# Moving two scatters of token numbers behind an early gather in a fused attention, SwiGLU and top-1 mixture-of-experts kernel

## The chip, the cores and the metric

The kernel runs on one core of a Trainium2 chip. The metric is device time in microseconds (us); lower is better. Before the change three runs took 1044.61, 1042.28 and 1041.61 us, so the median is 1042.28 us.

## The reference

Three layers follow one another: causal attention with a cumulative decay (4 batches, 8 heads, 576 positions, 64 per head), a SwiGLU layer on 2304 tokens of width 512 with 1536 inner columns, and a mixture of 8 experts in which each token goes to one expert. What matters here is the third:

```python
def _moe2_ref(x, w_gate, w1, w2):
    logits = x @ w_gate
    expert_idx = np.argmax(logits, axis=1)
    ...
    gate_w = probs[np.arange(N), expert_idx]
    for e in range(E):
        mask = expert_idx == e
        ...
        xe = x[mask]
        h = np.maximum(xe @ w1[e], 0.0)
        ye = h @ w2[e]
        out[mask] = gate_w[mask, None] * ye
```

## The kernel before

Phase 1 computes attention and, in between, the SwiGLU layer in nine groups of 256 tokens (`NG` = 9, group numbers 0 to 8). A group has six units. A unit `u` is `unit_g` (24 matmuls into `g`), `unit_v` (24 matmuls into `v`), and, one unit later, `unit_o` (12 matmuls into `yp`). Between them ScalarE makes `t` (L514) and `hi` (L530), VectorE makes `t` (L517, L524), and GpSimd makes `lo` (L531), which the last matmuls of `unit_o` read.

When a group is complete, `fin0` copies `yp` to `ys` and writes it to the DRAM table `y_d` (L562), `fin1` turns it, and `fin2` finds each token's expert and its rank there. `fin2` adds the token's number to a table `ixf` of 320 places per expert (three tiles of 128, 128 and 64 places). Tokens beyond 320 go to an overflow list `id_d` in DRAM: `fin2` computes places `pos` (L726) and token numbers `tid` (L728), and `put_ids` (L736) stores them with two indirect DMAs from GpSimd (L738), one for each half of the group. Places beyond the table's end are dropped by the bounds check. `pos` and `tid` are tiles of the pool `rt`, which has one buffer for each name, so the next group's `tid` has to wait until the scatters have read the last one's.

After `fin2` of group 7 (`NG - 2`), expert 0's first tile of 128 tokens is known. `early_tile` (L966) converts its 128 token numbers to `ix0` (L969) and gathers their rows from `y_d` into `xg` with an indirect DMA from GpSimd (L1051). Two units later, in the midst of the last unit's `v` matmuls, TensorE transposes those rows into `px` (L1062), and the last group's `fin1` and `fin2` are filled with expert 0's matmuls on that tile (`filler`, L990).

Phase 2 then runs the experts one by one: gathers of the token rows (L1051), first matmul (L1177), second (L1220), scatter to the output (L983). Weights come in pieces of 512 KB through four buffers `wr` (load L939 on the queue of SP, split on ScalarE L948 and VectorE L949 into a high and a low part).

The order of instructions on each engine is set by the framework's scheduler from the order of the code and a time model. `tc.keep_in_program_order` and `tc.issue_after` bind an instruction to its place, or to a place behind another instruction. GpSimd, like each engine, works through its own list in order: an instruction that waits holds all behind it. The second scatter of a pair waits until the first has landed, because both write `id_d`.

For the last group (8) the scatters are put off: `pos` and `tid` are copied to tiles of the pool `x0` (L731, L732) and stored in phase 2 (L1337).

Of the kernel before, what the change touches and what calls it, by code (L numbers as in the profile page):

```python
# [11 lines left out]
I32 = mybir.dt.int32  # L12
# [3 lines left out]
ALU = mybir.AluOpType  # L16
# [11 lines left out]
def kernel(  # L28
# [25 lines left out]
    NG = NT // G  # L54
# [4 lines left out]
    NSLOT = NE * OVS  # L59
    MAXOV = (NT - CAP + 127) // 128  # L60

    vec, act, pe, sp, gp = nc.vector, nc.scalar, nc.tensor, nc.sync, nc.gpsimd
# [417 lines left out]
    last = {}  # L480
# [135 lines left out]
    def fin2(g):  # L616
        yt, lg = ytp.pop(g)
        ps = ps_s.tile([128, 512], F32, tag="s", name="ps")
        for kk in range(KD):
            pe.matmul(  # L620
                out=ps[32 * kk:32 * kk + 32, 0:G], lhsT=rg[:, kk, :], rhs=yt[:, :, kk, :], start=True, stop=True,
# [6 lines left out]
        for i in range(2):  # L628
            pe.matmul(
                out=ps[:, NE * i:NE * i + NE], lhsT=lgp[:, 128 * i:128 * i + 128], rhs=sel, start=True, stop=True,  # L630
                skip_group_check=True,
            )
        rt = M["rt"]
# [7 lines left out]
        for i in range(2):  # L641
            vec.scalar_tensor_tensor(
                out=oh0[:, i, :], in0=lgv[:, i, :], scalar=mx[:, i, :], in1=desc, op0=ALU.is_ge, op1=ALU.mult
# [5 lines left out]
        for c0, m, i, first, last_ in (  # L649
# [4 lines left out]
                out=rk[:, c0:c0 + NE], lhsT=m, rhs=oh[:, i, :], start=first, stop=last_, skip_group_check=True  # L654
# [3 lines left out]
        for i in range(2):  # L658
            vec.tensor_tensor_reduce(
                out=junk[:, i, :], in0=cnt, in1=oh[:, i, :], scale=1.0, scalar=0.0, op0=ALU.mult, op1=ALU.add,  # L660
# [4 lines left out]
        for i in range(2):  # L665
            vec.tensor_tensor_reduce(
                out=junk[:, i, :], in0=rk[:, NE * i:NE * i + NE], in1=oh[:, i, :], scale=1.0, scalar=cs[:, i, :],
# [13 lines left out]
            out=eq, in0=slotc.rearrange("p (o s) -> p o s", o=1).to_broadcast([128, 2, NT3]),  # L681
# [4 lines left out]
            out=ra, in0=iota.rearrange("p (o t) -> p o t", o=1).to_broadcast([128, 2, 128]),  # L686
# [35 lines left out]
        )  # L722
        vec.tensor_tensor(out=pb_, in0=pb_, in1=rank, op=ALU.add)
        vec.tensor_tensor(out=pb_, in0=pb_, in1=ov_, op=ALU.mult)
        pos = rt.tile([128, 2, 1], I32, tag="pos", name="pos")
        vec.tensor_single_scalar(out=pos, in_=pb_, scalar=float(NSLOT), op=ALU.add)  # L726
        tid = rt.tile([128, 2], I32, tag="tid", name="tid")
        vec.tensor_single_scalar(out=tid, in_=tokm[:, 2 * g:2 * g + 2], scalar=float(NT), op=ALU.add)  # L728
        if g == NG - 1:
            EP["ids"] = [EP["x0"].tile([128, 2], I32, name=x) for x in ("pos8", "tid8")]  # L730
            vec.tensor_copy(out=EP["ids"][0], in_=pos.rearrange("p i o -> p (i o)"))  # L731
            vec.tensor_copy(out=EP["ids"][1], in_=tid)  # L732
        else:
            put_ids(pos.rearrange("p i o -> p (i o)"), tid)

    def put_ids(pos, tid):  # L736
        for i in range(2):
            gp.indirect_dma_start(  # L738
                out=id_d[:, :], out_offset=bass.IndirectOffsetOnAxis(ap=pos[:, i:i + 1].bitcast(U32), axis=0),
                in_=tid[:, i:i + 1], in_offset=None, bounds_check=NSLOT - 1, oob_is_err=False,  # L740
            )
# [331 lines left out]
    def unit(u, between=None):  # L1073
        if u < NU:
            t = unit_g(u)
            if between:
                between()
            unit_v(u, t)
        if u > 0:
            if u - 1 < NJ:  # L1080
                upto(markw[u - 1])
            unit_o(u - 1)
            g1, j1 = divmod(u - 1, NJ)
            if g1 == NG - 1 and j1 < len(EP["w2"]):
                EP["w2"][j1]()
                if j1 == len(EP["w2"]) - 1:
                    EP["w1"] = [go() for go in load_w(1, 1, w1[1])]
            if j1 == NJ - 1:
                if g1 == 0:
                    sg.close()  # L1090
                    M.update(routing_pools())
                fin0(g1)
                if g1 == NG - 1:
                    fill.append(filler())
                late.extend([(u + 1, fin1, g1), (u + 2, fin2, g1)])
        for x in list(late):
            if x[0] <= u or u == NU:
                x[1](x[2])
                late.remove(x)
                if x[1] == fin2 and x[2] == NG - 2:  # L1100
                    early_tile()
                    late.append((u + 2, lambda xs: transp(xts[0], 0, xs, lambda _: ps_x.tile(
                        [128, 512], F32, tag="x", name="px"
                    )), EP["xs"]))
# [212 lines left out]
    for s in range(NE + 1):  # L1317
        nxt = s + 1 if s < NE else None
        if s == 2:
            table()  # L1320
            reg["e"] = nc.values_load(
                tabi[0:1, 0, 0:1], engines=[mybir.EngineType.SP], min_val=0, max_val=NE - 1
            )
            reg["r"] = nc.values_load(
                tabi[0:1, 1, 0:1], engines=[mybir.EngineType.SP], min_val=0, max_val=NSLOT - 128
            )
            sp.dma_start(out=ixo, in_=id_d[bass.ds(reg["r"], 128), :])
            gp.indirect_dma_start(
                out=gwo, out_offset=None, in_=g_d[:, :],
                in_offset=bass.IndirectOffsetOnAxis(ap=ixo.bitcast(U32), axis=0),  # L1330
            )
        if nxt is not None:
            xgs[nxt] = fetch_x(nxt)
        if s == 1:
            pos_l = ix_p.tile([128, 2], I32, name="pos_l")
            tc.keep_in_program_order(vec.tensor_copy(out=pos_l, in_=EP["ids"][0]))
            put_ids(pos_l, EP["ids"][1])  # L1337
        live = [go() for go in weights(nxt, 1)] if nxt is not None and s else []
        if s < NE:
            h = ht_p.tile([128, KF2, 2 * CAP], F32R, tag="h", name="h")  # L1340
            for fk in range(KF2):
                mm1(fk, wt[s, 1], xts[s % 2], bank, h, 0 if s else 128)
                if fk >= 4 and live:
                    live.pop(0)()
        for f_ in live:
            f_()
        live = [go() for go in weights(nxt, 2)] if nxt is not None else []
        if nxt is not None:
            if nxt == 1:
                transp(xts[1], 0, xgs[1], bank)  # L1350
            else:
                turn(xts[nxt % 2], xgs[nxt])
        if nxt == NE:
            h_ov = [
                x.rearrange("p k c -> p (k c)")[:, 0:1024].rearrange("p (k c) -> p k c", k=KF2) for x in xts[s % 2]
            ]
            hs = hs_p.tile([128, KD, CAP], F32, tag="hs", name="hs").rearrange("p k c -> p (k c)")[:, 0:1024]
            mm1s(wt[NE, 1], xts[NE % 2], bank, hs, *h_ov)
        todo = [(t, n, idx) for t, (_, n, idx) in enumerate(xgs[s]) if s or t]
        for t, n, idx in todo:  # L1360
            mm2(t, n, idx, gate(s, t), wt[s, 2], *((h, h[:, :, LO:]) if s < NE else h_ov), bank, o_p)
            if live:
                live.pop(0)()
        for f_ in live:
            f_()
# [4 lines left out]
    with tc.tile_pool(name="lw", bufs=1) as lw, tc.tile_pool(name="lr", bufs=3) as lr, tc.tile_pool(  # L1370
        name="lx", bufs=1
# [67 lines left out]
```

## Time and profile before

| | us |
|---|---|
| median of three runs | 1042.28 |
| the profiled execution, its time | 1036.55 |
| its span from the first to the last instruction | 1034.8 |
| TensorE busy in it | 885.4 (86%) |
| GpSimd busy in it | 397.6 (38%) |
| last units of phase 1, routing and early tile | 726 to 777 |

Times in the rows are microseconds from the span's start. A row of a timeline has the start, the length, the engine, the line and the operation, and in brackets the idle time of its engine just before it with what ended it. PE is TensorE, PEld its weight load, DVE VectorE, ACT ScalarE, POOL GpSimd, SP the engine whose queue issues plain DMAs. An indirect DMA's row on POOL is the time in which GpSimd writes it out; its data land later. Ends of matmuls are modelled, so neighbouring rows overlap a little.

### The profile page before, as it was taken

What the parts mean: (1) busy time and instruction counts of PE and PEld (TensorE: products, weight loads), DVE (VectorE), ACT (ScalarE), POOL (GpSimd) and SP (SyncE); (2) the same over time, 40 slices, a digit from 0 to 9 for tenths busy, and PEclk for the clock granted to TensorE, in tenths of its full rate; (3) what the DMA queues carried; (4) which work ended last, traced back from release to release, by engine and by line L of the source; (5) the groups of instructions that cost most, each with busy time, mean ns of one, the idle gap of its engine ahead of it and who ended that gap; (6) DMA issues with size and microseconds to landing.
All of it is one profiled execution on the core that took longest, in us unless ns stands there. A gap on an engine that the chain in (4) does not pass through costs nothing.

```text
span 1034.8 us, 19815 instructions
## 1 busy us (share of the span) xinstructions
PE 885.4 (86%) x7003; PEld 738.0 (71%) x7029; DVE 632.2 (61%) x1829; ACT 558.0 (54%) x1208; POOL 397.6 (38%) x473
## 2 busy tenths in 40 slices
PE   1545557989889988899899999999789899999995
PEld 0333436867667776788688878888668799899894
DVE  6999879497577575567765443234326787656440
ACT  5987988476576565556554231213225455555441
POOL 1567767364255234344444222222225643111101
PEclk9995557999999998999999999999898899999998
DMA  8897997258776768566754440203329987754430
GB/s 241 201 225 209 227 193 167 85 131 156 139 154 142 168 113 161 115 110 150 105 109 108 113 123 2 41 2 83 51 35 219 273 239 214 207 170 152 149 104 33
DMA packets 314409, 145.30 MB, mean 140 GB/s; under 512 B 279649, under 2 KB 292065, under 8 KB 314308
## 3 DMA queue, kind: packets, MB, share of 16 engines
q1 hardware_dynamic: 310016, 133.63, 55.7%
q0 software_dynamic: 4096, 10.24, 3.9%
q8 instruction: 56, 0.92, 0.4%
q14 instruction: 45, 0.37, 0.2%
q10 hardware_dynamic: 196, 0.14, 0.1%
HBM read 81.62 MB, written 10.31 MB: 89 GB/s over the span
## 4 chain that ended last, share of the span: by engine, by line
PE 42%; DMA 7%; issue 6%; ACT 3%; DVE 2%; POOL 2%; SPq 1%; POOLq 0%; DVEq 0%; ACTq 0%
PE bank L1220 9%; PE bank L1177 8%; PE yp L544 8%; PE v L491 7%; PE g L491 6%; DMA pair<-yt 1%; DMA out_dram<-o,ix 1%; POOL xg L1051 1%; PE px L381 1%; DMA qkt<-qks 1%; DMA pt<-p 1%; DMA pair<-words 1%; ACT st L321 1%; DMA wr<-in_moe_w_dram 1%; DVE st L311 1%
## 5 line engine op out<-in xcount | busy, mean ns | idle before, releaser
L491 PE MATMUL v<-xr,wv 128*128 128x256 f16 x1296 | 162.4, 281 | 0.0
L491 PE MATMUL g<-xr,wg 128*128 128x256 f16 x1296 | 161.4, 278 | 0.5 <-DMA xr<-xs 0.5
L491 PEld LDWEIGHTS <-wg 128*128 128x128 f16 x1296 | 123.6, 100 | 26.8 <-issue 9.2
L491 PEld LDWEIGHTS <-wv 128*128 128x128 f16 x1296 | 128.9, 101 | 18.9 <-issue 1.0
L346 POOL TENSOR_TENSOR p<-st,p 128x128 f16<-128x128 f32 (+3 forms) x128 | 108.7, 854 | 79.1 <-issue 52.4
L531 POOL TENSOR_TENSOR lo<-t,hi 128x512 fp32r<-128x512 f32 x54 | 71.5, 1324 | 148.6 <-ACT hi L530 123.4
L321 ACT ACTIVATE st<-st,nb,c 128x64 f32<-128x64 f32 (+4 forms) x160 | 102.6, 643 | 1.2
L381 PE MATMUL px<-vs,pt 128*128 128x64 f16 x1280 | 58.7, 203 | 41.0 <-DMA pt<-p 30.0
L343 DVE CAST p<-st 128x64 f16<-128x64 f32 (+4 forms) x160 | 71.8, 464 | 30.7 <-ACT st L321 21.9
L381 PEld LDWEIGHTS <-pt 128*128 128x128 f16 x1280 | 52.4, 106 | 52.4 <-DMA pt<-p 35.1
L514 ACT ACTIVATE t<-g,gscale 128x512 f32<-128x512 f32 (+3 forms) x72 | 39.3, 571 | 75.5 <-PE g L491 75.5
L256 PE MATMUL ps<-qkt 128*128 128x64 f16 (+2 forms) x192 | 56.7, 311 | 25.9 <-DMA qkt<-qks 11.3
L357 POOL TENSOR_TENSOR p<-st,p 128x64 f16<-128x64 f32 (+1 forms) x128 | 54.2, 425 | 61.5 <-DVE p L343 30.6
L1220 PE MATMUL bank<-whi,h 128*128 128x512 f32 x200 | 66.9, 400 | 4.8 <-ACT h L1182 4.8
L983 POOL DMA_INDIRECT out_dram<-o,ix x24 | 26.6, 1110 | 113.8 <-ACT o L1222 71.2
L311 DVE CUSTOM_DVE_ANT_0 st<-ps,zero 128x64 f32<-128x64 f32 (+3 forms) x160 | 55.6, 376 | 24.2 <-PE ps L264 21.0
L517 DVE SCALAR_TENSOR_TENSOR t<-t,g 128x512 f32<-128x512 f32 x54 | 36.9, 684 | 54.3 <-ACT t L514 54.2
L530 ACT ACTIVATE hi<-t 128x512 fp32r<-128x512 f32 x54 | 33.8, 625 | 60.8 <-DVE t L524 60.8
L949 DVE TENSOR_TENSOR wlo<-wr,whi 128x1024 fp32r<-128x1024 f32 x48 | 57.7, 1245 | 14.1 <-ACT whi L948 12.3
L257 PE MATMUL ps<-qkt 128*128 128x64 f16 (+2 forms) x192 | 59.9, 315 | 0.0
L544 PE MATMUL yp<-wohi,hi 128*128 128x512 f32 x144 | 59.7, 414 | 0.0
L1177 PE MATMUL bank<-xh,whi 128*128 128x320 f32 (+1 forms) x192 | 58.9, 309 | 0.5 <-ACT xh L93 0.5
(300 smaller groups left out, 2274.2 us busy)
## 6 DMA issues: line engine op xcount, KB each, us to landing
wr<-in_moe_w_dram SPq DMA_DIRECT2D x72, 512.0 KB
vr<-in_v_dram SPq DMA_DIRECT2D x16, 288.0 KB
qk_in<-in_q_dram SPq DMA_DIRECT2D x32, 128.0 KB
qk_in<-in_k_dram SPq DMA_DIRECT2D x32, 128.0 KB
v_in<-in_v_dram SPq DMA_DIRECT2D x32, 128.0 KB
y_d<-ys SPq DMA_DIRECT2D x6, 512.0 KB
wg<-in_moe_w_gate_dram SPq DMA_DIRECT2D x5, 512.0 KB
raw<-in_moe_w_val_dram SPq DMA_DIRECT2D x5, 512.0 KB
```

What stands on the lines that cost most here:

```text
L257: pe.matmul(out=ps[:, o:o + n], lhsT=lq, rhs=qkt[:, 2, k0:k1], start=False, stop=False, skip_group_check=True)
L311: vec.tensor_tensor_reduce(out=sts[m][:, k0 - 64:k1 - 64], in0=ps[:, o:o + n], in1=zero.to_broadcast([128, n]), scale=1.0, scalar=init, op ...
L321: act.activation(out=sts[m], in_=sts[m], func=ACTF.Exp, scale=c[:, 0:1], bias=nb[:, m:m + 1], accum_out=sm[:, m, hh:hh + 1],)
L343: vec.tensor_copy(out=flat[:, o + 64:o + 64 + n], in_=src)
L346: gp.tensor_tensor(out=flat[:, o1:o1 + n - 64], in0=src[:, 64:n], in1=flat[:, o + 128:o + 64 + n], op=ALU.subtract)
L381: pe.matmul(out=px[:, 128 * m + 64 * hh:128 * m + 64 * hh + 64], lhsT=pm[:, o + ph * last + c, :], rhs=vs[:, hh, c, vh, :], start=(c == 0 ...
L491: pe.matmul(out=ps[:, fi, :], lhsT=w16[:, j, kk, wi, 128 * fi:128 * fi + 128], rhs=xr[:, kk, x0:x0 + 2, xi, :], start=(n_ == 0), stop=(n_ ...
L531: last["lo"] = gp.tensor_tensor(out=lo, in0=t, in1=hi.bitcast(F32), op=ALU.subtract)
L544: pe.matmul(out=yps[g][i], lhsT=hx[:, fi, 128 * i:128 * i + 128], rhs=wo[fk][wx], start=(j == 0 and n_ == 0), stop=(j == KF // 2 - 1 and n ...
L949: (eng or vec).tensor_tensor(out=l_, in0=t, in1=h_.bitcast(F32), op=ALU.subtract)
L1177: pe.matmul(out=p, lhsT=w[wi][:, kk, 128 * fk:128 * fk + 128], rhs=x[xi][:, kk, c0:CAP], start=(n_ == 0), stop=(n_ == 3 * KD - 1),)
L1220: pe.matmul(out=p[0:m, :], lhsT=hx, rhs=wx, start=(n_ == 0), stop=(n_ == len(prods) - 1))
```

## The change

For groups 7 and 8, `pos` and `tid` get tiles of their own in the pool `x0` and are no longer copied. Group 7's `put_ids` is no longer called in `fin2`, but after `fin0` of group 8, and bound behind the last `lo` of phase 1.

```diff
-        pos = rt.tile([128, 2, 1], I32, tag="pos", name="pos")
-        vec.tensor_single_scalar(out=pos, in_=pb_, scalar=float(NSLOT), op=ALU.add)
-        tid = rt.tile([128, 2], I32, tag="tid", name="tid")
+        held = g >= NG - 2
+        pos, tid = [
+            EP["x0"].tile([128, 2], I32, name=f"{x}{g}") if held else rt.tile([128, 2], I32, tag=x, name=x)
+            for x in ("pos", "tid")
+        ]
+        vec.tensor_single_scalar(
+            out=pos.rearrange("p (i o) -> p i o", o=1), in_=pb_, scalar=float(NSLOT), op=ALU.add
+        )
         vec.tensor_single_scalar(out=tid, in_=tokm[:, 2 * g:2 * g + 2], scalar=float(NT), op=ALU.add)
-        if g == NG - 1:
-            EP["ids"] = [EP["x0"].tile([128, 2], I32, name=x) for x in ("pos8", "tid8")]
-            vec.tensor_copy(out=EP["ids"][0], in_=pos.rearrange("p i o -> p (i o)"))
-            vec.tensor_copy(out=EP["ids"][1], in_=tid)
+        if held:
+            EP["ids", g] = (pos, tid)
         else:
-            put_ids(pos.rearrange("p i o -> p (i o)"), tid)
+            put_ids(pos, tid)
...
                 fin0(g1)
                 if g1 == NG - 1:
+                    with tc.issue_after(last["lo"].ins):
+                        put_ids(*EP["ids", NG - 2])
                     fill.append(filler())
...
-            tc.keep_in_program_order(vec.tensor_copy(out=pos_l, in_=EP["ids"][0]))
-            put_ids(pos_l, EP["ids"][1])
+            tc.keep_in_program_order(vec.tensor_copy(out=pos_l, in_=EP["ids", NG - 1][0]))
+            put_ids(pos_l, EP["ids", NG - 1][1])
```

On GpSimd, from the last copies of group 7 to the gathers of phase 2 (`lo` is a unit's low part, `id_d` a scatter of token numbers, the first `xg` the early tile's gather, the later ones those of phase 2), the list before reads:

```order
L531 TENSOR_TENSOR lo<-t,hi 128x512 x3
L738 DMA id_d<-tid,pos 16384x1 x2
L531 TENSOR_TENSOR lo<-t,hi 128x512
L1051 DMA xg<-y_d,ix_9793 128x512
L1237 IOTA thr 1x128
L1242 IOTA ii 1x128
L531 TENSOR_TENSOR lo<-t,hi 128x512
L1051 DMA xg<-y_d,ix 128x512
L1051 DMA xg<-y_d,ix 64x512
```

The same stretch of GpSimd's list with the change (three to five lines further down in the file):

```order
L531 TENSOR_TENSOR lo<-t,hi 128x512 x4
L1054 DMA xg<-y_d,ix_9787 128x512
L1242 IOTA thr 1x128
L1247 IOTA ii 1x128
L531 TENSOR_TENSOR lo<-t,hi 128x512
L741 DMA id_d<-tid_9783,pos_9782 16384x1 x2
L1054 DMA xg<-y_d,ix 128x512
L1054 DMA xg<-y_d,ix 64x512
```

The two scatters have left the place in front of the fourth `lo` and the early gather, and stand behind the fifth `lo`, in front of the first gather of phase 2.

On VectorE, around the conversion of the early tile's token numbers (`ix`) at the end of group 7's `fin2`, the list before reads:

```order
L717 TENSOR_TENSOR ixf<-ixf,rk 128x48
L969 CAST ix_9793<-ixf 128x1
L972 COPY gw_9796<-ixf 128x1
L728 TENSOR_SCALAR tid<-tokm 128x2
L732 COPY tid_10218<-tid 128x2
L949 TENSOR_TENSOR wolo<-wr,wohi 128x1024
L517 SCALAR_TENSOR_TENSOR t<-t,g 128x512
```

The same place of VectorE's list with the change:

```order
L717 TENSOR_TENSOR ixf<-ixf,rk 128x48
L972 CAST ix_9787<-ixf 128x1
L975 COPY gw_9790<-ixf 128x1
L952 TENSOR_TENSOR wolo<-wr,wohi 128x1024
L517 SCALAR_TENSOR_TENSOR t<-t,g 128x512
```

The last group's `tid` and its copy are gone from here; both held `tid` now stand some 170 instructions earlier on VectorE, around the `memset` of `xg` (L1049 before), and the copy of `pos` (L731) is gone too. The lists of TensorE, ScalarE and SP hold the same instructions in the same order.

## Rows read from the trace of the kernel before

**Rows 1.** Page, part 1: busy time, share of the span and instructions of each engine.
```profile
PE 885.4 (86%) x7003; PEld 738.0 (71%) x7029; DVE 632.2 (61%) x1829; ACT 558.0 (54%) x1208; POOL 397.6 (38%) x473
```

**Rows 2.** Waits of TensorE, 726 to 780: us in total, times, longest us.
```profile
PE px L1062 <- DMA xg<-y_d,ix: 6.7, 1, 6.7
PE bank L1062 <- DMA xg<-y_d,ix: 4.1, 1, 4.1
```

**Rows 3.** Timeline of TensorE, last unit's `v` and the early transposes.
```profile
738.50 2.02 PE L491 MATMUL v<-xr,wv 128*128 128x256 f16 x17
747.21 1.12 PE L1062 MATMUL px<-ident,xg 128*128 128x128 f32 x4 [6.70 <-DMA xg<-y_d,ix]
```

**Rows 4.** Timeline of GpSimd, 726 to 770.
```profile
730.71 1.05 POOL L738 DMA_INDIRECT id_d<-tid,pos  x1 [3.16 <-DVE eq L680]
739.94 0.97 POOL L738 DMA_INDIRECT id_d<-tid,pos  x1 [8.18 <-DMA id_d<-tid,pos]
740.93 1.28 POOL L531 TENSOR_TENSOR lo<-t,hi 128x512 fp32r<-128x512 f32 x1
742.37 1.06 POOL L1051 DMA_INDIRECT xg<-y_d,ix  x1 [0.16 <-issue]
...
751.42 1.27 POOL L531 TENSOR_TENSOR lo<-t,hi 128x512 fp32r<-128x512 f32 x1 [0.98 <-ACT hi L530]
769.18 0.98 POOL L1051 DMA_INDIRECT xg<-y_d,ix  x1 [16.49 <-DVE cnt L706]
```

**Rows 5.** The chain that ended last, in order of time: start, us, what.
```profile
713.01 2.62 PE v L491 x24
715.63 2.76 PE yp L544 x12
...
742.37 4.79 DMA xg<-y_d,ix
...
747.21 1.12 PE px L1062 x4
748.33 1.49 PE v L491 x7
749.82 7.10 PE yp L544 x24
...
757.70 2.83 DMA y_d<-ys
```

**Rows 6.** Timeline of VectorE, 734 to 750.
```profile
734.62 0.15 DVE L969 CAST ix<-ixf 128x1 int32<-128x1 f32 x1
...
744.03 0.17 DVE L728 TENSOR_SCALAR tid<-tokm 128x2 int32<-128x2 f32 x1 [9.20 <-DMA id_d<-tid,pos]
...
744.31 1.22 DVE L949 TENSOR_TENSOR wolo<-wr,wohi 128x1024 fp32r<-128x1024 f32 x1
745.45 0.68 DVE L517 SCALAR_TENSOR_TENSOR t<-t,g 128x512 f32<-128x512 f32 x1
749.00 0.69 DVE L93 TENSOR_TENSOR xl<-px,xh 128x512 fp32r<-128x512 f32 x1 [2.87 <-ACT xh L93]
```

**Rows 7.** Timeline of ScalarE, 733 to 740.
```profile
733.63 0.63 ACT L530 ACTIVATE hi<-t 128x512 fp32r<-128x512 f32 x1 [2.66 <-DVE t L524]
736.06 1.06 ACT L948 ACTIVATE wohi<-wr 128x1024 fp32r<-128x1024 f32 x1 [1.81 <-PE yp L544]
```

**Rows 8.** Stretches: length, busy us of each engine, PEclk (granted clock), DMA share, GB/s.
```profile
716.00:720.00 4.00, 4.00 (x30) 2.77 (x29) 2.23 (x4) 1.86 (x3) 1.27 (x1) 1.00 0.45 131
...
730.00:739.00 9.00, 9.00 (x71) 7.70 (x70) 2.88 (x14) 2.61 (x4) 1.05 (x1) 1.00 0.57 58
...
747.21:752.95 5.74, 5.74 (x19) 4.63 (x20) 1.44 (x2) 1.23 (x2) 1.80 (x3) 0.50 0.22 78
772.73:776.92 4.19, 0.07 (x1) 0.03 (x1) 0.18 (x1) 0.44 (x1) 3.06 (x4) 1.00 0.58 128
776.92:783.80 6.88, 6.40 (x31) 5.89 (x31) 4.88 (x6) 5.55 (x8) 4.37 (x4) 0.51 0.83 244
```

## The prediction

> **What bounds the kernel now.** I read the page first: TensorE is busy for 885.4 us, 86% of the span [rows 1], so time can be won only where it stands still or runs slowly. The list of TensorE's waits between 726 and 780 then shows two holes, 6.7 us before the early tile's transposes and 4.1 us before those of phase 2, both ended by a gather's landing [rows 2]. The change touches the first. TensorE's timeline places it: 17 of the 24 `v` matmuls of the last unit end at 738.50 + 2.02 = 740.52, and the transposes that stand next in its list start at 747.21 [rows 3].
>
> Why the gather is late stands in GpSimd's timeline [rows 4]. The first scatter is written out at 730.71 to 731.76; the second waits 8.18 us for its landing and is written at 739.94 to 740.91; the `lo` behind it runs from 740.93, and the gather follows at 742.37. The chain of waits takes the same way: gather 4.79 us from issue to landing, transposes, `v`, 24 `yp`, `ys`, and the write of `y_d` [rows 5]. The gather's own input was ready long before: `ix` was converted at 734.62 to 734.77 [rows 6]. So the scatters, which nobody needs soon, hold up a gather on which TensorE stands.
>
> The hole has a second price. The granted clock was 0.50, the level of 1.2 GHz, through the 5.74 us after it [rows 8]. The chain shows this in durations: 24 `yp` took 7.10 us there, where 12 took 2.76 at full clock, and 7 `v` took 1.49 where 24 took 2.62 [rows 5].
>
> **The change part by part.** *Scatters out of the gather's way.* GpSimd's list now has `lo`, `lo`, gather. The `lo` in front of the gather needs `hi`, which ScalarE ends at 733.63 + 0.63 = 734.26 [rows 7]. With 0.1 us to pass on, 1.28 us of `lo` and the 0.16 us before the gather [rows 4], the gather is issued at about 735.8 instead of 742.37: 6.6 us earlier. With the same 4.79 us [rows 5] it lands at 740.6, and TensorE is there at 740.52. Of the hole of 6.7 us about 0.1 is left.
>
> *The clock.* Without the hole I expect full clock. From the transposes to the end of the 24 `yp` TensorE took 1.12 + 1.49 + 7.10 = 9.71 us [rows 5]; half of 5.74 us, that is 2.87, was the low clock [rows 8]; 6.84 is left. Check: 24 `yp` at 2.76/12 are 5.52, 7 `v` at 2.62/24 are 0.76, four transposes at half of 1.12 are 0.56, together 6.84.
>
> *What is late next.* The last `lo`, which the second dozen of `yp` reads from its third matmul on. Before, it ran at 751.42 to 752.69, 2.87 us after `v` ended at 749.82 [rows 4, 5], under the slow first dozen. At full clock `v` ends only 0.76 us after the transposes, and `xl` (ScalarE's `xh`, then 0.69 us, ending 1.36 us after the transposes' end at 748.33 [rows 5, 6]) is ahead of `t` on VectorE: the chain starts 0.6 us later, and `lo` ends some 3.45 us after `v`. TensorE wants it 2.76 + 0.46 = 3.22 after `v`. I charge 0.2 us. The end of `yp` is then 740.6 + 6.84 + 0.2 = 747.6, instead of 749.82 + 7.10 = 756.92: **9.3 us** earlier.
>
> *VectorE.* Before, the last group's `tid` waited 9.20 us for the second scatter to land (until 744.03), and the weight split and `t` behind it stood too, `t` until 745.45 [rows 6]. That wait is gone, and so are the copies. It was hidden under TensorE's hole, so it counts nothing by itself; had it stayed, it would now show. The two early `tid` stand beside a `memset` that waited for its memory anyway; they cost at most two instructions of 0.17 us [rows 6], and I take 0.1 us off for them: 9.2 us.
>
> *The weight load behind the split.* The split of 1.22 us [rows 6] now runs at 737.1 (end of `wohi` [rows 7]) to 738.4, so SP's next load of 512 KB starts at about 738.4, not at 745.5. It meets the tail of the gather, as it did before, some 3 us after the gather's issue in both. I charge nothing; its bound stands under the rivals.
>
> *Scatters in their new place.* They start behind the last `lo`, at about 745.4. The first takes 1.05 us, lands 4 us (second scatter: 739.94 to 744.03 [rows 4, 6]) to 9.0 us (first: 730.71 to 739.71 or a little more [rows 4]) after issue, and the second takes 0.97: GpSimd is free at 750.5 to 755.5. The gather of phase 2 behind them waited 16.49 us for the last group's routing on VectorE, until 769.18 [rows 4]; 9.2 earlier this is 760.0. The cover holds with 4.5 us or more to spare. The `y_d` write of 2.83 us [rows 5] then runs at 748.5, beside the scatters; were it as slow as the load that ran beside the first scatter (58 GB/s over 730 to 739, against 131 at 716 to 720 [rows 8]), it would land at about 757, still before 760.0.
>
> *Two rules of the Trainium skill.* VectorE was idle from 734.83 to 744.03 while the gather was written [rows 4, 6], and with the change it is idle from 734.83 to 737.1, so the writing at 735.8 to 736.9 falls into idle time again. The Trainium skill, "SBUF — State Buffer", section "SBUF: two separate sides", says that GpSimd cannot write descriptors while VectorE runs certain copies; should the split of 1.22 us fall on the writing, the gather would land at 741.8 and the gain be 8.0 instead of 9.2. No row here shows such a lock. The early gather took 4.79 us for 256 KB [rows 5]. The Trainium skill, "DMA: Bandwidth & Descriptors", section "Anatomy of one DMA — SWDGE (gpsimd) path", gives about 2 us plus the bytes at 436 GB/s, an estimate of 2.6 us; by it the gather would land at 738.4, TensorE would not wait at all, and the gain would be 9.3. The measurement decides.
>
> **The sum.** All behind `yp` (the last group's routing, the next gathers, phase 2) starts from that end and moves with it; the lists of TensorE, ScalarE and SP are unchanged. So 1034.8 becomes 1025.6 in the span, and the profiled execution's 1036.55 becomes 1027.3. The median of the runs stood 5.7 us above that execution; I take the same gain there: 1042.28 - 9.2 = **1033.1 us**. A difference of 0.3%, 3.1 us, is about what a measurement of this kernel can tell from none.
>
> **The rivals.**
>
> *The gather lands late.* Against me: the gather issued at 769.18 released TensorE only at 776.92, 7.7 us later [rows 4, 8], though more gathers stood behind it; and the first scatter took 9.0 us while a weight load ran beside it. With 7.7 us it lands at 743.5, TensorE stands 3.0 us, and `yp` ends at 750.5: gain 6.4 if the clock stays high, 3.5 if 2.87 us of low clock come back. With 9.0 us it is 5.1 or 2.2. The middle is 4.3: **1038.0 us**. For me: the only early gather on record took 4.79, alone as it will be now.
>
> *The gain is given back at the next hole.* The second hole of 4.19 us was followed by 6.88 us at 0.51 [rows 8], which cost some 3.4 us. The low stretches behind the two holes differ, 5.74 and 6.88 us, the longer one behind the shorter hole. Moved by 9.2 us, the second low stretch may be longer or shorter by its own 3.4 us; and a gather of phase 2 may be released by something that does not move. Together these might give back 7 us: **1040 us**. Against: everything that the chain shows behind `yp` hangs on it.
>
> *The scatters hold up phase 2: slower.* They now stand directly in front of the gathers for which TensorE has its second hole. GpSimd must reach those at 760.0 and starts the scatters at 745.4. Past 12.6 us of landing each further us is a us of TensorE; past 21.8 the gain is gone, past 25 the kernel is slower by 3 us: **1046 us**. The slowest landing on record is 9.0 us, so this needs something that no row shows.
>
> **How the numbers follow.** Forecast 0.70; late gather 0.19, of which 0.13 is still faster by over 3.1 us; given back 0.07, of which 0.03; slower 0.04. Faster by over 0.3%: 0.86; within: 0.10; slower: 0.04. Range: the low end is the gain of 9.2 and a second low stretch shorter by its 3.4 us, 1029.7, less the 0.7 us by which the fastest run lies under the median, 1029.0; the high end is the late gather's 2.2, 1040.1.
>
> **What would show it.** Right: the gather on GpSimd at about 735.8, directly behind a `lo`; TensorE's wait before the early transposes under 1 us; granted clock 1.00 from 740 to 756; 24 `yp` in about 5.7 us; no `tid` waiting for a scatter at 744; the scatters at 745 to 756, and the first gather of phase 2 still released by VectorE's `cnt`, at about 760. Wrong: a wait of 3 us or more at the transposes; low clock between 740 and 756; or that gather released by `id_d`.

## The result and the profile after

The changed kernel took 1030.64 us, the median of four runs (1026.6 to 1034.63), beside 1041.94 us for the kernel before on the same chip, also four runs: a ratio of 0.9895 with a 95% interval of [0.9854, 0.9935]. Measured again later on with six runs beside eleven, it was 1030.71 against 1037.1 us, 0.9928 [0.9893, 0.9963]. The prediction was 1033.1 us in a range of 1029.0 to 1040.1, a ratio of 0.9912. Both intervals hold it, and both lie wholly below 0.997. The medians differ by 11.3 us in the first measurement and by 6.4 us in the second, so the time confirms the direction and the rough size; the size itself is read from the stage below. A ratio leaves out slow runs, over 1.5% above the fastest of their kernel (two of six in experiment 10), while a median counts all runs, so the two need not agree to the last digit.

The profiled execution took 1030.24 us, its span 1028.4. The page's first part, the busy time of each engine, answers to [rows 1]: TensorE is as busy as before, so most of the time came from its idle stretches.

```profile
PE 886.6 (86%) x7029; PEld 734.9 (71%) x7029; DVE 628.4 (61%) x1827; ACT 558.4 (54%) x1208; POOL 395.9 (38%) x473
```

TensorE's waits between 728 and 772 answer to [rows 2]. The wait of 6.7 us at `px` (now L1065) is gone, the one before phase 2 has stayed:

```profile
PE bank L1065 <- DMA xg<-y_d,ix: 4.3, 1, 4.3
```

TensorE's timeline answers to [rows 3]: the transposes follow the 17 `v` with no idle time, and `yp` ends where the first L1002 starts, at 749.25.

```profile
740.67 2.02 PE L491 MATMUL v<-xr,wv 128*128 128x256 f16 x17
742.52 0.60 PE L1065 MATMUL px<-ident,xg 128*128 128x128 f32 x4
742.96 0.93 PE L491 MATMUL v<-xr,wv 128*128 128x256 f16 x7
743.64 0.70 PE L544 MATMUL yp<-wo,hi 128*128 128x512 f32 x2
...
749.25 0.40 PE L1002 MATMUL p<-whi,xh 128*128 128x512 f32 x1
```

GpSimd's timeline answers to [rows 4]. The gather stands directly behind a `lo`, both scatters behind the last `lo`, and the first gather of phase 2 still waits for `cnt`:

```profile
728.43 1.29 POOL L531 TENSOR_TENSOR lo<-t,hi 128x512 fp32r<-128x512 f32 x1 [6.31 <-ACT hi L530]
736.57 1.29 POOL L531 TENSOR_TENSOR lo<-t,hi 128x512 fp32r<-128x512 f32 x1 [6.84 <-ACT hi L530]
738.01 1.08 POOL L1054 DMA_INDIRECT xg<-y_d,ix  x1
...
745.95 1.29 POOL L531 TENSOR_TENSOR lo<-t,hi 128x512 fp32r<-128x512 f32 x1 [1.44 <-ACT hi L530]
747.40 1.03 POOL L741 DMA_INDIRECT id_d<-tid,pos  x1 [0.16 <-issue]
752.07 0.98 POOL L741 DMA_INDIRECT id_d<-tid,pos  x1 [3.64 <-DMA id_d<-tid,pos]
761.68 0.98 POOL L1054 DMA_INDIRECT xg<-y_d,ix  x1 [8.64 <-DVE cnt L706]
```

VectorE's timeline answers to [rows 6]. No `tid` waits here; the idle time in front of the weight split is ScalarE's `wohi`:

```profile
736.78 0.15 DVE L972 CAST ix<-ixf 128x1 int32<-128x1 f32 x1
...
739.32 1.23 DVE L952 TENSOR_TENSOR wolo<-wr,wohi 128x1024 fp32r<-128x1024 f32 x1 [2.32 <-ACT wohi L951]
741.65 0.69 DVE L517 SCALAR_TENSOR_TENSOR t<-t,g 128x512 f32<-128x512 f32 x1 [1.10 <-ACT t L514]
```

The stretches (length, busy time of each engine, granted clock, DMA share, GB/s) answer to [rows 8]: from the transposes to near the end of `yp`, then the remaining hole, then what follows it.

```profile
742.52:748.30 5.78, 5.78 (x33) 4.81 (x32) 1.35 (x2) 1.23 (x2) 2.73 (x4) 1.00 0.18 68
764.90:769.10 4.20, 0.43 (x5) 0.32 (x3) 0.18 (x1) 0.69 (x1) 3.03 (x4) 0.99 0.47 87
769.00:775.80 6.80, 5.70 (x27) 5.21 (x28) 4.09 (x5) 5.04 (x7) 3.89 (x4) 0.50 0.89 240
```

**How two traces are laid over each other.** In this execution all of the last units came 2.16 us later than in the one before, though no instruction of those units had changed: the third-last `lo` of phase 1 started at 728.43, before at 726.27. (In the second profiled execution of the same kernel it started at 730.02, so a shift of this size lies between executions.) So what is compared below is the **stage** from that `lo` to the first gather of phase 2. Before it took 769.18 - 726.27 = 42.91 us, after 761.68 - 728.43 = 33.25: 9.66 us less. From the same `lo` to the span's end it is 308.53 and 299.97, 8.6 us less; in the profiled execution of the second measurement 298.28, 10.3 us less.

### The profile page after: what moved, and what is told of

Read it like the earlier page. It is cut to its first block, busy times and chain, and to the rows that moved or that the text cites. A ratio compares the mean times of both kernels' runs of the same rounds, so it can differ in the third digit from the quotient of the medians.

```text
span 1028.4 us, 19836 instructions
## 1 busy us (share of the span) xinstructions
PE 886.6 (86%) x7029; PEld 734.9 (71%) x7029; DVE 628.4 (61%) x1827; ACT 558.4 (54%) x1208; POOL 395.9 (38%) x473
## 5 line engine op out<-in xcount | busy, mean ns | idle before, releaser
L491 PE MATMUL g<-xr,wg 128*128 128x256 f16 x1296 | 159.2, 275 | 1.7 <-DVE t L517 1.2
L491 PEld LDWEIGHTS <-wg 128*128 128x128 f16 x1296 | 122.9, 99 | 27.5 <-issue 10.3
L531 POOL TENSOR_TENSOR lo<-t,hi 128x512 fp32r<-128x512 f32 x54 | 71.5, 1325 | 152.0 <-ACT hi L530 128.5
L343 DVE CAST p<-st 128x64 f16<-128x64 f32 (+4 forms) x160 | 68.7, 445 | 30.2 <-ACT st L321 20.7
L1225 PE MATMUL bank<-whi,h 128*128 128x512 f32 x200 | 67.4, 402 | 4.1 <-ACT h L1187 4.1
L259 PE MATMUL ps<-cum,nc 128*128 128x64 bf16 (+2 forms) x192 | 59.8, 317 | 0.0
L544 PE MATMUL yp<-wohi,hi 128*128 128x512 f32 x144 | 59.7, 415 | 0.0
```

Source lines behind the costliest of these rows:

```text
L259: pe.matmul(out=ps[:, o:o + n], lhsT=pk, rhs=cum3[:, k0 - 64:k1 - 64], start=False, stop=(k1 <= d0), skip_group_check=True,)
L343: vec.tensor_copy(out=flat[:, o + 64:o + 64 + n], in_=src)
L491: pe.matmul(out=ps[:, fi, :], lhsT=w16[:, j, kk, wi, 128 * fi:128 * fi + 128], rhs=xr[:, kk, x0:x0 + 2, xi, :], start=(n_ == 0), stop=(n_ ...
L531: last["lo"] = gp.tensor_tensor(out=lo, in0=t, in1=hi.bitcast(F32), op=ALU.subtract)
L544: pe.matmul(out=yps[g][i], lhsT=hx[:, fi, 128 * i:128 * i + 128], rhs=wo[fk][wx], start=(j == 0 and n_ == 0), stop=(j == KF // 2 - 1 and n ...
L1225: pe.matmul(out=p[0:m, :], lhsT=hx, rhs=wx, start=(n_ == 0), stop=(n_ == len(prods) - 1))
```

## The experiments

Twelve kernels ran. Their stage is read from GpSimd's timeline, like that of the change. The kernel before took 1042.63 us (median) beside 1 to 4, 1038.19 beside 5, 6, 8 and 9, and 1037.1 beside 7 and 10 to 12; kernels 3 to 6 and 8 ran once and are judged by the stage, not by the time. Each stage is that of one profiled execution.

**1. Tiles alone.** The change without its move: `pos` and `tid` have tiles of their own, group 7's scatters stay in `fin2`.

```diff
-        if held:
-            EP["ids", g] = (pos, tid)
-        else:
-            put_ids(pos, tid)
+        if held:
+            EP["ids", g] = (pos, tid)
+        if g < NG - 1:
+            put_ids(pos, tid)
...
-                    with tc.issue_after(last["lo"].ins):
-                        put_ids(*EP["ids", NG - 2])
```

> Own tiles for the last two groups' places, but group 7's scatters stay in front of the early gather. I measure the stage from the start of the `lo` that is third-last in phase 1 (726.27 before, 728.43 after) to the first gather of phase 2 (769.18, 761.68): 42.9 us before, 33.25 after. Hole theory (all the gain is the early gather's place on GpSimd): TensorE still waits 6 to 7 us at the early transposes, the clock falls, the stage is 42 to 43 us and the time that of before within 0.3%, although VectorE's wait of 9.20 us for `tid` is gone. Rival (VectorE's wait and the copies were part of the price): stage 36 to 41 us, time 2 to 7 us below before.

Measured: 1047.1 us, ratio 1.0044 [1.0018, 1.0069], a little slower than before. GpSimd's timeline shows why:

```profile
732.03 1.05 POOL L741 DMA_INDIRECT id_d<-tid,pos  x1 [3.16 <-DVE eq L680]
744.00 0.98 POOL L741 DMA_INDIRECT id_d<-tid,pos  x1 [10.92 <-DMA id_d<-tid,pos]
...
746.43 1.06 POOL L1054 DMA_INDIRECT xg<-y_d,ix  x1 [0.16 <-issue]
```

The scatters still stand in the way, and the first kept the second waiting 10.92 us here, against 8.18 before [rows 4]. TensorE's wait for the gather is longer by 3.1 us:

```profile
PE px L1065 <- DMA xg<-y_d,ix: 9.8, 1, 9.8
```

The stage is 44.68 us, 1.8 us longer than before and not 3.1, because TensorE's granted clock was back at 0.96 from 754.50 on, 2.9 us after the transposes began; before, it stayed at 0.50 for 5.74 us behind the hole [rows 8]. That the tiles alone bring nothing was expected; the loss of 0.4% was not. The trace shows 1.8 us, from the scatter's slower landing in this one execution, the fastest of ten; the interval begins at 1.9 us, and whether anything else adds to it stays open.

**2. The move alone.** The kernel before, with group 7's scatters behind the last `lo`, but `pos` and `tid` still in the pool with one buffer.

```diff
+        elif g == NG - 2:
+            EP["ids7"] = (pos.rearrange("p i o -> p (i o)"), tid)
         else:
             put_ids(pos.rearrange("p i o -> p (i o)"), tid)
...
+                    with tc.issue_after(last["lo"].ins):
+                        put_ids(*EP["ids7"])
```

> Group 7's scatters moved as in the change, but places in the shared single buffers with the copies of group 8, as before. Hole theory: the stage is 33 to 34 us as with the change, time 9 to 11 us below before; VectorE's `tid` waits somewhere for the scatters but under TensorE's work. Rival (the tiles of their own are needed): the last group's `pos` or `tid` waits on VectorE for the second scatter's landing, stage 35 to 39 us, time 5 us or more above the changed kernel.

Measured: 1038.38 us, 0.9957 [0.9926, 0.9989], stage 41.96, longer than either theory had it, though by the rival's mechanism. The early hole is gone, and another has come: VectorE's `tid` of the last group must wait until the moved scatters have read the tile, and the copy `yt` (L610) stands behind it. VectorE's timeline:

```profile
759.21 0.17 DVE L728 TENSOR_SCALAR tid<-tokm 128x2 int32<-128x2 f32 x1 [6.88 <-DMA id_d<-tid,pos]
759.42 0.17 DVE L732 COPY tid<-tid 128x2 int32<-128x2 int32 x1
759.49 0.68 DVE L610 COPY yt<-ps 128x512 f32<-128x512 f32 x1
```

TensorE's waits of the same kernel show the new hole:

```profile
PE ps L620 <- DVE yt L610: 5.0, 1, 5.0
```

Its stretch from 762 to 767, behind that hole, has the granted clock at 0.50:

```profile
762.00:767.00 5.00, 5.00 (x15) 4.10 (x14) 1.55 (x15) 0.21 (x1) 0.00 (x0) 0.50 0.03 0
```

So the two parts of the change need each other: in the stage the tiles alone lose 1.8 us and the move alone gains 0.95, together they gain 9.66; in the time it is 0.4% lost, 0.4% won, together 0.7 to 1.1% won. The interval of the move alone reaches down to 1.1 us, so time and stage need not disagree.

**3. No scatters of group 7.** The change without the two moved scatters. This leaves out group 7's part of the overflow list.

```diff
-                    with tc.issue_after(last["lo"].ins):
-                        put_ids(*EP["ids", NG - 2])
```

> Group 7's token numbers are not stored at all (that part of the overflow list is left out), else as the change. Hole theory with a full cover: the scatters cost nothing where they now stand, stage 33.2 us within 0.4, time within 4 us of the changed kernel. Rival (the scatters still cost something in front of phase 2, by GpSimd or by the DMA engines): stage 32.5 us or less, and the wait of 4.3 us before the transposes of phase 2 shorter by 0.5 us or more.

Measured: 1028.88 us in one run, stage 33.43 against 33.25. GpSimd waits 14.46 us for `cnt` instead of 8.64; the gather comes no sooner. In their new place the scatters cost the stage nothing.

**4. Directly behind the gather.** The scatters stand behind the early gather, in front of the last `lo`.

```diff
-                    with tc.issue_after(last["lo"].ins):
-                        put_ids(*EP["ids", NG - 2])
...
+                    with tc.issue_after(last["xg"].ins):
+                        put_ids(*EP["ids", NG - 2])
```

> Group 7's scatters directly behind the early gather, in front of the last `lo`, not behind it. Hole theory: the gather is as early as with the change, no hole at the early transposes; but the second scatter waits 3.6 to 8 us for the first to land, so the last `lo` starts 1 to 6 us later than 17.5 us after the stage's start, TensorE waits for it in the last `yp`, stage 34 to 39 us. Rival (only the gather's place counts, any place behind it is free): stage 33.2 us within 0.4.

Measured: 1035.56 us, stage 37.05. GpSimd's timeline: the last `lo` comes at 750.91, 19.8 us into the stage instead of 17.5.

```profile
742.09 2.04 POOL L741 DMA_INDIRECT id_d<-tid,pos  x1 [0.31 <-issue]
749.40 0.98 POOL L741 DMA_INDIRECT id_d<-tid,pos  x1 [5.27 <-DMA id_d<-tid,pos]
750.91 1.25 POOL L531 TENSOR_TENSOR lo<-t,hi 128x512 fp32r<-128x512 f32 x1
```

TensorE waits 2.0 us for it (`yp L544 <- POOL lo L531`), and behind this short hole its granted clock fell to 0.51 for 3.4 us:

```profile
753.40:756.80 3.40, 3.40 (x10) 2.70 (x9) 0.69 (x1) 0.60 (x1) 0.00 (x0) 0.51 0.04 14
```

The hole of 2.0 us and half of the 3.4 make 3.7 us, and the stage is 3.8 us longer. Behind the gather is not enough: the scatters must stand behind the last `lo` too.

**5 and 6. The gather late on purpose.** Two, then four multiplications of zeros on GpSimd in front of the gather.

```diff
+                for _ in range(2):
+                    gp.tensor_tensor(out=x, in0=x, in1=EP["gw"].to_broadcast([128, DM]), op=ALU.mult)
```

> The change, with two idle multiplications of 128x512 zeros on GpSimd (about 1.3 us each) put in front of the early tile's gather, so that it is issued about 2.6 us later; the result is the same. Theory (the gather's landing ends the hole before the early tile's first transpose): it was ready with 0 us of wait after the change, so a hole of 1.5 to 2.6 us comes back there, and the stretch from the third-last `lo` of phase 1 to the first gather of phase 2 grows from 33.25 to about 35 to 36 us; without low clock behind it the price is the hole alone. Rival (the hole came from the order on TensorE or from `tid`, and the gather has slack): no hole, stretch 33 to 34 us. One look: time some 1 to 3 us over the change, which one look can hardly tell, so the stretch decides.

> As the run before, with four such multiplications: the gather about 5.2 us later, some 1.5 us earlier than in the kernel before by its own stage. Theory: a hole of 4 to 5.2 us, and if a hole of that length brings the low clock back in phase 1's last group, another 2 to 3 us beside it: stretch 37.5 to 42 us (42.91 in the kernel before). If the clock stays high: 37 to 38.5 us. Rival (the gather has slack): under 35 us.

Measured: 1032.46 and 1031.99 us, stages 33.24 and 34.31. Neither theory was tested as meant. The scheduler saw the added work and placed the transposes later in TensorE's list, in the midst of the last 24 `yp`; the gather, 2.25 and 5.3 us later, was met there. In the second kernel TensorE's timeline shows a hole of 0.85 us:

```profile
744.75 0.66 PE L1067 MATMUL px<-ident,xg 128*128 128x128 f32 x4 [0.85 <-DMA xg<-y_d,ix]
```

In its stretch of 7.2 us behind that the clock stayed at 1.00:

```profile
744.80:752.00 7.20, 7.20 (x40) 5.75 (x44) 2.08 (x3) 1.86 (x4) 1.33 (x2) 1.00 0.21 73
```

The gather was issued at 741.04 there, so it landed 3.7 us after issue. The runs gave a better question: is it enough to move the transposes?

**7. Only the transposes later.** The kernel before with one number changed, which puts the four transposes behind the first dozen of the last 24 `yp`. GpSimd's list stays as it was.

```diff
-                    late.append((u + 2, lambda xs: transp(xts[0], 0, xs, lambda _: ps_x.tile(
+                    late.append((NU, lambda xs: transp(xts[0], 0, xs, lambda _: ps_x.tile(
```

> The kernel before with one thing changed: the early tile's four transposes stand behind the first dozen of the last 24 `yp` in TensorE's list, not in front of the last seven `v` (VectorE's last `t` L524 then stands in front of `xl`). GpSimd's list is as before, so the gather is issued as late as before, 16.1 us after the third-last `lo`, and lands 4.8 us later. Theory (the hole is the time between TensorE's arrival at the transposes and that landing, wherever they stand): TensorE arrives 0.76 + 2.76 = 3.5 us later, so the hole is about 3.1 us instead of 6.7; behind it the last `lo`, which waits for VectorE's `tid`, costs about 0.5 us; stretch from the third-last `lo` to the first gather of phase 2 about 37 us at full clock, 38 to 40 if a hole of 3 us brings the low clock, against 42.91 before and 33.25 with the change. Time 3 to 6 us below the kernel before. Rival (VectorE's 9.2 us behind `tid` would have shown anyway, or low clock comes all the same): a hole of 5 us or more for `lo` or `t`, stretch over 40 us, time within 0.3% of before.

Measured: 1033.38 us, 0.9954 [0.9910, 0.9998], stage 37.72. TensorE's waits:

```profile
PE px L1062 <- DMA xg<-y_d,ix: 2.8, 1, 2.8
```

It also waited twice for a `lo`, as its timeline shows:

```profile
740.66 0.50 PE L544 MATMUL yp<-wo,lo 128*128 128x512 f32 x1 [0.74 <-POOL lo L531]
747.77 0.50 PE L544 MATMUL yp<-wo,lo 128*128 128x512 f32 x1 [0.16 <-POOL lo L531]
```

The hole shrank to 2.8 us, about as worked out (3.1), and no low clock followed (TensorE's stretch from 745.50 to 752.50 at 1.00). The 0.74 us are GpSimd's: that `lo` ran at 739.32, directly behind the second scatter. VectorE's `tid` waited 9.7 us as before, and of that only the 0.16 us at the last `lo` showed. A step in the order of the waiting engine alone brought about half of the stage's gain, 5.2 of 9.66 us.

**8. Scatters three times.** The rival that ended on the slower side: scatters in the way of phase 2's first gather.

```diff
-                        put_ids(*EP["ids", NG - 2])
+                        for _ in range(3):
+                            put_ids(*EP["ids", NG - 2])
```

> The change, with the pair of scatters of group 7's token numbers issued three times in the new place (the same numbers to the same rows, so the result is the same). GpSimd waited 8.64 us for the count in front of the first gather of phase 2, and a pair takes about 4.7 us from issue to issue where the second waits for the first. Theory of the slower rival (scatters in the way of phase 2's first gather): two more pairs need some 9 to 10 us against 8.64 us of room, so the gather comes 0.5 to 3 us later: stretch 33.5 to 36 us, GpSimd's wait for the count gone and a wait for a scatter's landing in its place. Rival (there is far more room, as the scatters wait for nothing): stretch 33.25 plus or minus 0.4 us and a wait for the count of over 2 us left.

Measured: 1045.24 us, stage 48.61. GpSimd's timeline:

```profile
746.79 1.03 POOL L741 DMA_INDIRECT id_d<-tid,pos  x1 [0.16 <-issue]
751.39 0.98 POOL L741 DMA_INDIRECT id_d<-tid,pos  x1 [3.57 <-DMA id_d<-tid,pos]
756.59 0.99 POOL L741 DMA_INDIRECT id_d<-tid,pos  x1 [4.22 <-DMA id_d<-tid,pos]
766.75 0.98 POOL L741 DMA_INDIRECT id_d<-tid,pos  x1 [9.17 <-DMA id_d<-tid,pos]
769.66 0.98 POOL L741 DMA_INDIRECT id_d<-tid,pos  x1 [1.93 <-DMA id_d<-tid,pos]
775.15 0.98 POOL L741 DMA_INDIRECT id_d<-tid,pos  x1 [4.51 <-DMA id_d<-tid,pos]
776.44 0.98 POOL L1054 DMA_INDIRECT xg<-y_d,ix  x1 [0.30 <-issue]
```

The gather no longer waits for `cnt` but stands behind the scatters, and TensorE's hole before phase 2 is 19.5 us long. So the rival's mechanism is real, and its cover is about what the profile said: from the second scatter to the sixth there are 23.8 us, the stage grew by 15.4, so 8.4 us were covered, of 8.64. My 0.5 to 3 us were far too small. I had counted two more waits of 4.7 us, but each scatter waits for the one before it, so there are four: 18.7 us, some 10 over the cover. The other 5 us came from one landing that took about 10 us, and not for other transfers: in the stretch that it ended in, the DMA share was 0.02 (the last but one figure).

```profile
760.00:770.00 10.00, 4.81 (x26) 3.99 (x24) 0.43 (x3) 0.69 (x1) 1.32 (x2) 0.88 0.02 1
```

**9. The first gathers of phase 2 alone.** A try to shorten the remaining hole: the second expert's gathers wait until the first expert's tiles are transposed.

```diff
-        if nxt is not None:
+        if nxt == 1:
+            mark_t = ix_p.tile([128, 1], F32, name="mark_t")
+            seen_x = gp.tensor_copy(out=mark_t, in_=xts[0][0][:, 0, CAP - 1:CAP].bitcast(F32))
+            with tc.issue_after(seen_x.ins):
+                xgs[nxt] = fetch_x(nxt)
+        elif nxt is not None:
             xgs[nxt] = fetch_x(nxt)
```

> The change, with the gathers of phase 2's second expert held back until the last transpose of the first expert's first tiles has been copied (a GpSimd copy of one column of that tile stands in front of them), so that the first gathers land with nothing issued behind them. The first gather of phase 2 landed 7.9 us after its issue with five more behind it, the early tile's alone in 4.1 us at most. Theory A (the gathers behind share its bandwidth): it lands 1.5 to 3.5 us sooner, the hole of 4.3 us before phase 2's first transposes shrinks by as much, and the time is 1.5 to 4 us below the change (1026.5 to 1029), if the second expert's gathers still land before they are wanted. Theory B (it lands late for another reason, or the second expert's gathers are then late): the hole stays within 0.7 us, or a new one comes before the second expert's transposes, and the time is within 0.3% of the change or above it.

Measured: 1033.11 us, 0.9957 [0.9933, 0.9981], no less than the change (0.9895 and 0.9928), with a stage of 33.27 us. The hole is 4.16 us. TensorE's timeline:

```profile
773.01 1.70 PE L1065 MATMUL bank<-ident,xg 128*128 128x128 f32 x8 [4.16 <-DMA xg<-y_d,ix]
```

The first gather was issued at 765.21 and let TensorE go 7.8 us later, with only the smaller second gather of its expert behind it; with the others behind it too, that took 7.9 us (761.68 to 769.62). Theory A falls: the second expert's gathers are not what slows it. (The early gather's "4.1 us at most" should have been 4.5, from 738.01 to 742.52.)

**10 and 11. The places before the filler.** The first gather of phase 2 waits for `cnt`, and VectorE's chain to it holds two splits of the filler. The first kernel puts both behind `rb`; the second puts them behind `rb` and `cnt` and the place matmuls in front of the filler's second matmuls.

```diff
-        step(g)
...
-        vec.tensor_tensor(out=rb[:, :, 0, :], in0=eq, in1=toks.to_broadcast([128, 2, NT3]), op=ALU.mult)
+        last["rb"] = vec.tensor_tensor(out=rb[:, :, 0, :], in0=eq, in1=toks.to_broadcast([128, 2, NT3]), op=ALU.mult)
+        step(g)
...
-            split(pair[0], pair[1], p, pair[0].bitcast(F32))
+            with tc.issue_after(last["rb"].ins): split(pair[0], pair[1], p, pair[0].bitcast(F32))
```

The second one besides, against the first:

```diff
-        step(g)
...
-        step(g)
...
-        vec.tensor_tensor(out=cnt, in0=cnt, in1=rk[:, 2 * NE:3 * NE], op=ALU.add)
+        last["cnt"] = vec.tensor_tensor(out=cnt, in0=cnt, in1=rk[:, 2 * NE:3 * NE], op=ALU.add); step(g); step(g)
...
+            with tc.issue_after(last["rb" if half == 0 else "cnt"].ins): split(pair[0], pair[1], p, pair[0].bitcast(F32))
```

> The change, with VectorE's two splits of the filler (`lo`, 0.69 us each) put behind the `rb` that the last group's places need; TensorE's two place matmuls L694 then stand behind two instead of eight filler matmuls L1033. In the trace of the change both splits lay between `rp` and `rb` (758.45 and 759.58). Theory: the first gather of phase 2 waits for this chain, so it comes sooner by 0.6 to 1.2 us (stretch 32.0 to 32.7 instead of 33.25; one split now stands in front of `ix`), and the filler's TensorE work ends up to 0.5 us later, inside the hole of 4.3 us; time 0.5 to 1 us less, which 5 rounds will hardly tell. Rival: the chain has slack, or the schedule of phase 2, which shifts with it in places, eats it: stretch 33.25 plus or minus 0.3, time the same or above.

> As the run before, but both splits behind `cnt`, and the place matmuls in front of all of the filler's second matmuls (one pair of them in front of the filler's transposes too). Theory: nothing of the filler is left in the chain, so the first gather of phase 2 comes 1.6 to 2.2 us sooner (stretch 31.0 to 31.7); TensorE waits some 1.6 us for `rb` early on, and the hole before phase 2's first transposes shrinks from 4.3 to 0.5 to 1 us, so that the sum of both is 2 us smaller: time 1 to 2 us below the change. Rival: the early wait and other shifts of phase 2's order cost what the sooner gather brings: same time as the change or above.

Measured: 1035.04 us, 0.9947 [0.9901, 0.9992], and 1031.64 us, 0.9950 [0.9919, 0.9980]; the change on the same chip 0.9928. The stages did shrink, to 32.33 and 31.93 us (32.0 to 32.7 and 31.0 to 31.7 expected), and in the second the hole before phase 2's first transposes is gone. In the first that hole was 3.6 us, and the waits for `h` in phase 2's second matmul added up to 9.1 us. The second kernel's waits from 750 to the end show where the gain went:

```profile
PE bank L1225 <- ACT h L1187: 6.5, 2, 3.7
PE rk L694 <- DVE rb L689: 1.9, 1, 1.9
PE bank L1225 <- DVE h L1189: 1.1, 2, 0.6
```

Here the waits for `h` add up to 7.6 us, against these in the change:

```profile
PE bank L1225 <- ACT h L1187: 4.1, 2, 3.9
```

What was gained ahead was given back at waits behind, and 1.9 us at `rb` came in addition. Neither kernel beats the change, and none of the twelve does beyond its interval.

**12. The change again.**

> The change itself, unaltered, beside the three others on the same chip, for a tighter interval: 0.9895 of the kernel before was measured with four runs, [0.9854, 0.9935]. By the trace its stretch is 9.66 us shorter and the span's end some 8.6 us earlier against the same start, so 0.991 to 0.992 is expected; a ratio over 0.995 would mean that the gain is lost behind the stretch in most executions.

Measured: 1030.71 us, 0.9928 [0.9893, 0.9963]; stage 763.28 - 730.02 = 33.26 us. The hole before phase 2 was 4.4 us. The gain of the stage holds.

## Why the prediction was right

**The hole.** Predicted: the gather at 735.8, landed at 740.6, 0.1 us of hole left. Measured in the time of before (2.16 us taken off): the gather at 735.85, and no wait. Four points lie within some 0.6 us of one line, on which the hole grows by as much as the gather is later: 18.85, 16.10, 16.33 and 9.58 us from the third-last `lo` to the gather gave holes of 9.8 (tiles alone), 6.7 (before), 2.8 (transposes 3.5 us later, 6.3 with them) and 0 (change). The hole is the time between TensorE's arrival at the transposes and the landing.

**The clock.** Predicted: 2.87 us back. The stretch stayed at 1.00, and 24 `yp` took 743.64 to 749.25 = 5.6 us, where 5.52 were worked out and 7.10 had been measured [rows 5].

**The last `lo`.** I charged 0.2 us; TensorE's list shows no wait for it. I had misread the order: the second dozen of `yp` reads `lo` from its fifth matmul on, not from its third. TensorE's timeline of the change shows the four `hi` that come first:

```profile
746.47 1.07 PE L544 MATMUL yp<-wo,hi 128*128 128x512 f32 x4
747.38 0.41 PE L544 MATMUL yp<-wo,lo 128*128 128x512 f32 x1
```

By my own sum TensorE then wants `lo` 2.76 + 4 * 0.23 = 3.68 us after `v`, and 3.45 was soon enough. The end of `yp` came at 747.1 in the time of before, against 747.6 predicted, and the stage gained 9.66 where the sum had 9.2. The difference is this charge and the 0.1 us for the two early `tid`, and the rest is near what a gather that landed within 4.5 us instead of 4.79 gives. The charges were small beside the gain, so the mechanism and not luck made the size right; that the median of the runs came within 2.5 us of the forecast is no finer a test than their scatter allows (1026.6 to 1034.63).

**VectorE's `tid`.** "Had it stayed, it would now show" is borne out only in part. In the kernel with later transposes it stayed in its old place, beside a hole of 2.8 us, and showed 0.16 us. In the move alone it had to wait for the scatters in their new place, and that showed: 5.0 us of hole and the low clock.

**The scatters' place.** Predicted: free at 750.5 to 755.5, the gather of phase 2 at 760.0 behind `cnt`. Measured in the time of before: the second scatter written out by 750.9, the gather at 759.5, still behind `cnt`.

**The rivals.** The late gather did not come. Which of its two branches would have come stays open: a hole of 2.8 us kept the full clock in the run with later transposes, while holes of 2.0 and 1.9 us at other places were followed by the low one (last section). The second hole was 4.3 us as before, with 6.8 us at 0.50 behind it, so nothing was given back there. The slower rival was rightly given little: its bound of 12.6 us of landing was about right, since 4.67 us of landing left 8.64 us of room (13.3 together).

**Two sentences of mine that the runs don't bear out.** I tied the slow first scatter (9.0 us) to the weight load beside it. The load may be part of it: from issue to issue the first scatter took 9.2, 9.4 and 12.0 us in the old place and 4.3 to 5.0 us in the new one, in nine executions. But with the scatters issued three times, one took from 756.59 to 766.75 with the DMA engines all but idle. And I wrote that no row here shows VectorE locking out the writing of descriptors; the trace of the kernel before held such rows, in phase 2 (last section).

## What to carry to other kernels

On an engine that works in order, stores that nobody waits for belong behind the last instruction that feeds the bottleneck, not only behind the one that is late; one place too early cost 3.8 of 9.7 us here. Before moving such a store, ask who else waits for it through its buffers: a tile with a single buffer carried the same wait to VectorE, and alone the move shortened the stage by 0.95 us of 9.66, the tiles by nothing. A late transfer can also be met by moving its consumer later, which here took one number and brought half of the stage's gain, and what a shorter stretch gains must be looked for again at the waits behind it.

## What the runs showed of the hardware

- **A split on VectorE holds up the writing of an indirect DMA that begins inside it.** In the run with the scatters directly behind the gather, the first scatter took 2.04 us to write instead of about 1.0. VectorE's timeline of that run has the weight split in exactly that time:

```profile
742.01 1.22 DVE L952 TENSOR_TENSOR wolo<-wr,wohi 128x1024 fp32r<-128x1024 f32 x1 [2.32 <-ACT wohi L951]
```

  The scatter started at 742.09; from the split's end at 743.23 to 744.13 are 0.9 us, a whole writing. The trace of the kernel before has the same in phase 2, in the timelines of GpSimd and VectorE:

```profile
816.16 1.20 DVE L949 TENSOR_TENSOR wolo<-wr,wohi 128x1024 fp32r<-128x1024 f32 x1
816.40 1.84 POOL L1051 DMA_INDIRECT xg<-y_d,ix  x1 [0.41 <-issue]
```

  In the fourteen traces 147 writings began inside a split that had 0.2 us or more to run. Of these, 133 ended 0.8 to 1.0 us after the split's end, two later still, and 12 that began within 0.02 us of the split's start were not held up (0.9 to 1.0 us). With VectorE idle a writing took 0.9 to 1.1 us. Beside `o` (L1225 before), where VectorE reads one operand from TensorE's output `bank`, 62 writings took 0.97 to 1.06 us, so not every VectorE operation does it. The Trainium skill, "SBUF — State Buffer", section "SBUF: two separate sides", describes such a lock for certain operations of VectorE and warns of it for a copy; that the split, which reads both operands from SBUF, does it too is what these rows show. In the change the gather was written from 738.01 to 739.09 and the split started at 739.32: it was missed by 0.2 us.
- **Landings of the same kind differ widely.** A scatter of 128 token numbers held up the next by 2.9 to 12.0 us from issue to issue, and one of 10.2 us came with the DMA engines all but idle. Where TensorE waited for it, the early gather of 256 KB let it go 3.7 to 5.3 us after its issue and the first of phase 2, of the same size, after 6.7 to 8.6 us, with more gathers behind it or not. Why stays open; no run here told it apart.
- **The low clock does not follow the length of the hole alone.** Holes of 9.8, 6.7, 5.0 and 4.3 us were followed by a granted clock of 0.50, the level of 1.2 GHz, but so were one of 2.0 us (scatters directly behind the gather, 0.51 over 753.4 to 756.8) and one of 1.9 us (in the run with both splits behind `cnt`, 0.61 on average over 757 to 765), while 2.8 us in the run with later transposes left it at 1.00. Nor did the longer hole leave more of it: 2.9 us behind 9.8, 5.7 us behind 6.7. A price for it is best taken from the row of the very stretch.
